# A new order, later stores, a second turning buffer and more exponentials on ScalarE in an attention-and-maxout kernel

## The chip, the cores and the metric

The kernel runs on one core of a Trainium2 chip. The core has a matrix engine (TensorE, PE in the profile, with PEld for its weight loads), three engines for elementwise work (VectorE or DVE, ScalarE or ACT, GpSimd or POOL), a queue engine that issues transfers (SyncE, SP) and 16 DMA engines. ACT can issue transfers too. The metric is the time of one execution in microseconds (us), as the median over runs.

## What is computed

Linear attention over 8 batches of 8 heads, 576 rows and 64 columns, and then a feed-forward layer on the 4608 x 512 result that takes the largest of three products:

```python
q_s = exp(q - max(q, axis=-1));  q_s /= sum(q_s, axis=-1) + 1e-09
k_s = exp(k - max(k, axis=2));   k_s /= sum(k_s, axis=2) + 1e-09
kv = einsum('bhsd,bhse->bhde', k_s, v)
x = einsum('bhsd,bhde->bhse', q_s, kv)          # rows b*576+s, columns h*64+e
h = maximum(maximum(x @ w1, x @ w2), x @ w3)    # 512 -> 768
out = h @ w_out                                 # 768 -> 512
```

## The kernel before

**Attention in pairs.** Two heads of one batch are a pair; pair n is batch n // 4 and heads 2(n % 4) and the next. There are 32. The first eight (batches 0 and 1) are turned by PE transposes (L533 to L558 for k, L713 for q). The other 24 are "late pairs". For one of these, k's column maximum is taken on DVE (L573 to L575), finished across partitions on POOL (L578), subtracted on DVE (L581), and exponentiated on ACT (L588). PE multiplies it with v (L603), and ACT writes the scaled 64 x 64 blocks to `bd` (L619). q arrives as `qt`, 128 x 576 with nine rows of 64 in each partition. DVE takes each row's maximum (L661), subtracts it (L663), ACT exponentiates all of it at once (L668), DVE adds up the rows (L670), inverts (L672, L673) and scales (L676). A block transpose on DVE writes `tb` (L681), and eight copies of 36 KB each by DMA put the blocks into `qT` (L694, some issued by SP and some by ACT). Then PE multiplies `qT` with `bd` (L740): this is the pair's product, a column block of x.

**The layer in stages.** Each fp32 weight is split into a high and a low fp32r part, and each product of the layer takes three matmuls of 128 x 512. The weights come in 24 slices, `wst` (L415), whose words are put together on DVE, POOL and ACT; the joined words are stored to DRAM as `wholes` (L462), and the split parts, which live in `gw`, as `scratch` (L1079 and L1084, three transfers for each of nine weight pairs: `kept`). The first three batches run as chunks of 512 rows with the weights in `gw` (L773, then L812). The other rows run as three double chunks with seven products where eight would be usual (L932, then L1043). Their weights are combinations: `sums` loads two `wholes` into `bench` (L1094), adds and subtracts on DVE (L1099, L1103) and stores to `scratch` (L1105). They come back one by one into a ring of 16 places in `gw` (L913). Their inputs are `raw` blocks of x, mixed on DVE and ACT (L869 to L880).

**What sets the order.** Nothing is scheduled by hand. Every piece of work is a generator of `Step`s with an engine, a cost and what it needs, frees and gives; `Streams.run` plays them on a model of the engines and takes, on each engine, the ready step of lowest rank. What it takes is issued in that order, and an engine then works through its list strictly in order. Constants near the top set ranks and model costs: `DMA_RATE` and `DMA_LANDS` for transfers, `AT`, `STEP`, `LATER` and so on for pairs, `SLICE…` for weights, `Q_BY_ACT` for the pairs whose row maximum goes into the exponential as ACT's bias. "turn" is the moment at which the first stage's buffers are given up and the late pairs' buffers exist.

## Time and profile before

| | |
|---|---|
| time, median of 3 runs | 708.24 us (700.74 to 711.59) |
| profiled execution, its own time | 706.54 us |
| its span, first to last instruction | 704.7 us |
| mean granted PE clock | 0.979 |
| DVE, ACT, POOL busy | 480.6, 264.1, 57.5 us |
| HBM read and written | 95.16 MB and 30.67 MB |

The profile is of one execution. Its engines' busy times are unions over instructions, and a matmul's own duration overlaps with that of the next, so PE's pace is read from how many matmuls fill a stretch, not from the mean of one. Releasers ("<-") say what ended a wait. "SPq" and "ACTq" are the issuing queues; a transfer's time to landing is counted from its issue. Eight semaphores go round among the transfers of SP and ACT, so a transfer also waits until the one that had its semaphore before has landed.

### The profile page before, as it was taken

How to read it: one execution, taken by the hardware profiler on the slowest of the kernel's cores; microseconds unless marked ns; L12 is line 12 of the kernel's file. 1: busy time of each engine (PE TensorE's matmuls, PEld its weight loads, DVE VectorE, ACT ScalarE, POOL GpSimd, SP SyncE). 2: the span in 40 equal slices, each digit the busy share in tenths (PEclk: the TensorE clock that was granted, in tenths of full speed). 3: DMA queues.
4: the chain of work that ended last, by engine and by line, in shares of the span. 5: the costliest groups of instructions: out<-in, count | busy, mean ns of one | idle time of the engine just before them, and what ended most of it. 6: DMA issues, size and time to landing. Idle time of an engine off the chain costs nothing.

```text
span 704.7 us, 9928 instructions
## 1 busy us (share of the span) xinstructions
PE 656.3 (93%) x3318; PEld 516.6 (73%) x3318; DVE 480.6 (68%) x865; ACT 264.1 (37%) x548; POOL 57.5 (8%) x68
## 2 busy tenths in 40 slices
PE   2859999999999788989988999999999999999997
PEld 1537877787777566767666777778888888888886
DVE  7988788589986778998868889624455913445421
ACT  4677855333443324453323336421112521111122
POOL 3222322110010000101000001000000000000000
PEclk9968999999999899999999999999999999999999
DMA  9999984416668976778878883346666316665012
GB/s 228 275 333 314 282 276 135 140 48 182 190 198 241 282 227 203 231 231 263 250 212 237 245 239 94 111 137 195 195 193 194 95 70 177 192 193 155 0 60 60
DMA packets 126162, 133.57 MB, mean 190 GB/s; under 512 B 57376, under 2 KB 88864, under 8 KB 124960
## 3 DMA queue, kind: packets, MB, share of 16 engines
q1 hardware_dynamic: 120800, 128.80, 62.0%
q10 hardware_dynamic: 5312, 4.16, 2.1%
q8 instruction: 26, 0.43, 0.3%
q14 instruction: 24, 0.20, 0.1%
HBM read 95.16 MB, written 30.67 MB: 179 GB/s over the span
## 4 chain that ended last, share of the span: by engine, by line
PE 73%; DMA 13%; DVE 6%; SPq 4%; ACT 2%; issue 1%; ACTq 0%; DVEq 0%
PE bank L932 33%; PE bank L773 18%; PE bank L1043 10%; DMA qT<-tb 6%; PE bank L812 4%; PE bank L740 3%; PE ps L603 2%; DMA wst<-in_moe_w_dram 2%; DVE tb L681 1%; DMA qt<-in_q_dram 1%; DMA vt<-in_v_dram 1%; DVE gw L880 1%; SPq L694 1%; DMA gw<-scratch 1%; DVE raw L876 1%
## 5 line engine op out<-in xcount | busy, mean ns | idle before, releaser
L932 PE MATMUL bank<-gw 128*128 128x512 f32 x1134 | 268.6, 395 | 3.0 <-ACT gw L878 1.1
L932 PEld LDWEIGHTS bank<-gw 128*128 128x128 f32 x1134 | 211.6, 188 | 51.6 <-issue 4.6
L773 PE MATMUL bank<-gw 128*128 128x512 f32 x432 | 112.6, 414 | 0.0
L773 PEld LDWEIGHTS bank<-gw 128*128 128x128 f32 x432 | 82.5, 195 | 21.5 <-issue 4.5
L1043 PE MATMUL bank<-oh,halves 128*128 128x512 f32 x288 | 89.2, 390 | 0.8 <-DVE halves L1021 0.8
L1043 PEld LDWEIGHTS bank<-oh,halves 128*128 128x128 f32 x288 | 54.1, 188 | 13.0 <-DVE halves L1021 1.2
L1043 PE MATMUL bank<-ol,halves 128*128 128x512 f32 x144 | 57.4, 398 | 0.0
L773 PE MATMUL bank<-x,gw 128*128 128x512 f32 x216 | 53.8, 403 | 0.0
L773 PEld LDWEIGHTS bank<-x,gw 128*128 128x128 f32 x216 | 40.1, 188 | 10.0 <-issue 1.4
L812 PE MATMUL bank<-oh,h 128*128 128x512 f32 x144 | 44.8, 393 | 0.0
L1021 DVE TENSOR_TENSOR halves<-hf,halves 128x768 fp32r<-128x768 f32 (+2 forms) x30 | 23.8, 798 | 30.1 <-ACT halves L1019 30.1
L578 POOL PARTITION_ALL_REDUCE kma<-km x24 | 20.0, 834 | 282.3 <-DVE ke L581 111.9
L740 PE MATMUL bank<-qT,bd 128*128 128x512 f32 x48 | 27.2, 650 | 15.8 <-DMA qT<-tb 11.9
L681 DVE STREAM_TRANSPOSE tb<-qt 128x576 f32<-128x576 f32 x24 | 30.4, 1265 | 7.0 <-DMA qT<-tb 4.6
L785 DVE TENSOR_TENSOR m<-bank,m 128x512 f32<-128x512 f32 x36 | 24.7, 686 | 11.4 <-PE bank L773 10.8
L812 PEld LDWEIGHTS bank<-oh,h 128*128 128x128 f32 x144 | 27.1, 188 | 6.8 <-issue 1.0
L812 PE MATMUL bank<-ol,h 128*128 128x512 f32 x72 | 32.0, 444 | 0.0
L1062 ACT COPY m<-bank 128x512 f32<-128x512 f32 x23 | 13.5, 586 | 48.9 <-PE bank L1043 40.1
L1043 PEld LDWEIGHTS bank<-ol,halves 128*128 128x128 f32 x144 | 27.0, 188 | 6.1 <-ACT qt L668 0.2
L989 ACT COPY m<-bank 128x512 f32<-128x512 f32 x18 | 10.5, 586 | 55.5 <-PE bank L932 45.4
L994 ACT COPY m<-bank 128x512 f32<-128x512 f32 x18 | 10.6, 587 | 55.3 <-PE bank L932 54.5
L996 DVE TENSOR_TENSOR m<-bank,m 128x512 f32<-128x512 f32 x18 | 12.4, 690 | 25.5 <-PE bank L932 21.4
(141 smaller groups left out, 876.3 us busy)
## 6 DMA issues: line engine op xcount, KB each, us to landing
gw<-scratch SPq DMA_DIRECT2D x189, 256.0 KB, 3.0
wst<-in_moe_w_dram SPq DMA_DIRECT2D x18, 512.0 KB, 5.8
scratch<-bench SPq DMA_DIRECT2D x9, 1024.0 KB, 4.9
out_dram<-m SPq DMA_DIRECT2D x32, 256.0 KB, 2.0
vt<-in_v_dram SPq DMA_DIRECT2D x56, 128.0 KB, 3.6
scratch<-gw SPq DMA_DIRECT2D x27, 256.0 KB, 4.8
qt<-in_q_dram SPq DMA_DIRECT2D x24, 288.0 KB, 3.7
kt<-in_k_dram SPq DMA_DIRECT2D x24, 256.0 KB, 4.0
```

The costliest lines, as they stand in the source:

```text
L578: nc.gpsimd.partition_all_reduce(kma, km, P, bass_isa.ReduceOp.max)
L603: nc.tensor.matmul(out=kv[r, :nv], lhsT=ke[rows, s, hh, :], rhs=self.vt[rows, hh, s, 0:nv], start=(s == 0), stop=(s == 4),)
L681: nc.vector.transpose(out=tb.rearrange("p e (c s) -> p s e c", s=QS), in_=self.qt.rearrange("p s (e c) -> p s e c", e=2))
L740: nc.tensor.matmul(out=xT, lhsT=self.terms[0], rhs=self.terms[1][:, cs], start=True, stop=True)
L773: nc.tensor.matmul(out=ps, lhsT=l[:, cc], rhs=r, start=(cc == 0 and t == 0), stop=(cc == NC - 1 and t == 2))
L785: nc.vector.tensor_max(out=m, in0=self.m.pop((j, i)), in1=m)
L812: nc.tensor.matmul(out=po, lhsT=l, rhs=r[:, j, :], start=(j == 0 and i == 0), stop=(j == NJ - 1 and i == 2))
L932: nc.tensor.matmul(out=po, lhsT=w[:, a, cc], rhs=x[:, b, cc], start=(first and cc == 0 and t == 0), stop=(cc == 1 and t == 2), skip_group_ ...
L996: nc.vector.tensor_sub(out=ma, in0=po("w"), in1=ma)
L1021: nc.vector.tensor_sub(out=hl, in0=src, in1=hh.bitcast(F32))
L1043: nc.tensor.matmul(out=po, lhsT=l, rhs=r[:, j, :], start=(j == 0 and i == 0), stop=(end and i == 2))
L1062: nc.scalar.copy(out=o, in_=po)
```

## The change

Costs and ranks of the planner are new numbers, and so the order of nearly every engine is new. Besides that, four things change in the code: (1) `kept` waits for "turn", so the 27 stores of split weights go out after the first stage instead of during it; (2) `tb` has two buffers instead of one; (3) k's maximum over its five row blocks is one reduction over a strided view instead of three maxima; (4) for the pairs in `Q_BY_ACT`, now 16 of them late pairs, q's negated row maximum goes to ACT as a bias, in nine calls that also give the row sums, so L663 and L670 fall away for them. Of the eight turned pairs six instead of three are done this way.

```diff
-DMA_LANDS = 2.0
-DMA_RATE, DMA_FIRST, DMA_AT_FIRST = 356.0, 0.62, 16.0
+DMA_LANDS = 1.8
+DMA_RATE, DMA_FIRST, DMA_AT_FIRST = 300.0, 0.74, 16.0
...
+LATE = (6.8, 43.0, 75.9, 91.3, 39.2, 63.1, 42.8, 12.9, 102.3, 84.5, 80.2, 91.4, 361.6, 375.8, 329.0, 379.5, 306.9, 342.2, 395.5, 316.4, 365.6, 408.8, 357.1, 341.6)
...
-FIRST_LOADS = 'vqwkQVKVwqvkQvkKqwqvwk'
+FIRST_LOADS = 'qVKKVqQwkwqvvQwvkqvkwk'
...
-Q_BY_ACT = (0, 4, 6)
+Q_BY_ACT = (1, 2, 4, 5, 6, 7, 8, 9, 11, 12, 13, 14, 17, 19, 20, 21, 22, 23, 26, 28, 30, 31)
...
-N_QT = 3
+N_QT, N_TB = 3, 2
+SPARE = 1.5
...
         def k_plain(self):
...
-            nc.vector.tensor_max(out=half, in0=kt[:, :, 0:2, :], in1=kt[:, :, 2:4, :])
-            nc.vector.tensor_max(out=kmv, in0=half[:, :, 0, :], in1=half[:, :, 1, :])
-            nc.vector.tensor_max(out=kmv, in0=kmv, in1=kt[:, :, 4, :])
+            nc.vector.tensor_reduce(
+                out=km.rearrange("p (h d) -> p h d", h=2), in_=kt.rearrange("p h s d -> p h d s"), op=ALU.max, axis=AX.X
+            )
...
-                nc.vector.tensor_reduce(out=qm, in_=rows3, op=ALU.max, axis=AX.X)
-                yield Step("V", dve(rows * D), port="V")
-                nc.vector.tensor_tensor(
-                    out=rows3, in0=rows3, in1=qm.unsqueeze(2).broadcast_to([P, rows, D]), op=ALU.subtract
-                )
+                nc.vector.tensor_reduce(out=qm, in_=rows3, op=ALU.max, axis=AX.X, negate=by_act)
+                if by_act:
+                    for s in range(0, QS, 3):
+                        yield Step("A", 3 * 0.33)
+                        for i in range(s, s + 3):
+                            nc.scalar.activation(
+                                out=rows3[:, i, :], in_=rows3[:, i, :], func=AF.Exp,
+                                bias=qm[:, i : i + 1], accum_out=qs[:, i : i + 1],
+                            )
...
-            tb = turn_pools[0].tile([P, 2, BL * QS], F32, name="tb", bufs=1)
+            tb = turn_pools[0].tile([P, 2, BL * QS], F32, name="tb", bufs=N_TB)
...
+            yield Step("-", SPARE, gives=("qT", n))
...
     def kept(f):
...
-        yield Step("S", 1.28, both, gives=("scratch", f, True, False, False), kb=512)
+        yield Step("S", 1.28, [*both, "turn"], gives=("scratch", f, True, False, False), kb=512)
```

`FIRST_LOADS` names the first transfers in order: a small letter is a pair's main rows of q, k or v, a capital the left-over rows of one or of three pairs, and `w` a weight slice. The first k of pair 0 was the fourth entry and is now the ninth.

**Where it shows: SP in the first stage.** Before, in the middle of the weight loads (`wst`) and of the loads for batch 1 (`kt`), stand stores of split weights (`scratch<-gw`), three by three:

```order
L462 DMA wholes_79<-m_441 128x512
L415 DMA wst_471<-in_moe_w2_dram 128x4x256
L1079 DMA scratch_78<-gw_73 128x2x256 x2
L1084 DMA scratch_78<-gw_73 128x2x256
L492 DMA kt1_91<-in_k_dram 128x4x64 x2
L415 DMA wst_547<-in_moe_w1_dram 128x4x256
L462 DMA wholes_79<-m_513 128x512
L1079 DMA scratch_78<-gw_73 128x2x256 x2
L1084 DMA scratch_78<-gw_73 128x2x256
```

Now they stand behind the last weight load, after "turn", around the first turned copies of pair 8 (`qT_1546`) and the loads of pairs 10 (`qt_1576`, `kt0`, `vt0`):

```order
L1110 DMA bench_1395<-wholes_79 128x1024
L1095 DMA scratch_78<-gw_73 128x2x256 x2
L1100 DMA scratch_78<-gw_73 128x2x256
L1095 DMA scratch_78<-gw_73 128x2x256 x2
L1121 DMA scratch_78<-bench_1395 128x2048
L1100 DMA scratch_78<-gw_73 128x2x256
L503 DMA kt0_90<-in_k_dram 128x2x256
L505 DMA kt0_90<-in_k_dram 64x2x64
L709 DMA qT_1546<-tb_1530 32x288 x4
L531 DMA qt_1576<-in_q_dram 128x576
L514 DMA vt0_92<-in_v_dram 128x4x64 x2
```

What moved are the 27 stores: 15 stand ahead of pair 8's turned copies on SP, 12 behind.

**SP at pair 14.** `qT_2221` is pair 14's turned q before. Ahead of its four copies on SP stand loads for other pairs, an output, two ring loads (`gw<-scratch`) and a load of 512 KB (`bench`):

```order
L506 DMA vt0_92<-in_v_dram 128x4x64 x2
L508 DMA vt0_92<-in_v_dram 64x2x64
L523 DMA qt_2173<-in_q_dram 128x576
L821 DMA out_0_dram<-m_2167 128x512
L495 DMA kt0_90<-in_k_dram 128x2x256
L497 DMA kt0_90<-in_k_dram 64x2x64
L913 DMA gw_73<-scratch_78 128x512 x2
L523 DMA qt_2215<-in_q_dram 128x576
L1094 DMA bench_1449<-wholes_79 128x1024
L694 DMA qT_2221<-tb_2207 32x288 x4
```

Now pair 14's is `qT_2244`, and its copies follow the first two ring loads at once:

```order
L709 DMA qT_2164<-tb_2145 32x288 x4
L837 DMA out_0_dram<-m_2177 128x512
L709 DMA qT_2164<-tb_2145 32x288 x2
L1121 DMA scratch_78<-bench_1395 128x2048
L514 DMA vt0_92<-in_v_dram 128x4x64 x2
L516 DMA vt0_92<-in_v_dram 64x2x64
L929 DMA gw_73<-scratch_78 128x512 x2
L709 DMA qT_2244<-tb_2232 32x288 x4
L531 DMA qt_2269<-in_q_dram 128x576
```

The q load and the 512 KB load that stood between ring loads and copies are gone from there.

**DVE at pair 14.** Before, from the row sums of pair 14 (`qt_2073`) to its block transpose (`tb_2207`), with steps of `sums` (`bench`) between:

```order
L670 TENSOR_REDUCE qs9_162<-qt_2073 128x9
L1099 TENSOR_TENSOR bench_1449<-bench_1449 128x256
L672 TENSOR_SCALAR qs9_162<-qs9_162 128x9
L673 RECIPROCAL qs9_162<-qs9_162 128x9
L1099 TENSOR_TENSOR bench_1449<-bench_1449 128x256
L676 TENSOR_TENSOR qt_2073<-qt_2073,qs9_162 128x576
L1099 TENSOR_TENSOR bench_1449<-bench_1449 128x256
L681 STREAM_TRANSPOSE tb_2207<-qt_2073 128x9x64
```

Now (`qt_2037`, `tb_2232`), the sums come from ACT and the subtraction has gone too:

```order
L687 TENSOR_SCALAR qs9_162<-qs9_162 128x9
L688 RECIPROCAL qs9_162<-qs9_162 128x9
L691 TENSOR_TENSOR qt_2037<-qt_2037,qs9_162 128x576
L620 TENSOR_SCALAR rk_2216<-ps_130 128x1
L621 RECIPROCAL rk_2216<-rk_2216 128x1
L667 TENSOR_REDUCE qm9_163<-qt_2162 128x9
L696 STREAM_TRANSPOSE tb_2232<-qt_2037 128x9x64
```

L670 has no counterpart for this pair, and three of `sums`' steps are no longer in between. The number of matmuls on PE is the same; of the layer's 2430, 390 stood ahead of pair 8's product and 411 do now, and from there to the product of pair 31 it was 1011 and is 1008.

More of the change, by code (lines that the diff above doesn't have):

```diff
@@ L47 @@
 N_TMP = 7
-SUMS_AT, SUMS_STEP = 60.0, 8.0
-LATER = 400.0
-N_QT = 3
+N_QT, N_TB = 3, 2
+SPARE = 1.5
 LEFT_OF = (0, 1, 6, 2, 3, 4, 5)
@@ L222, in issue @@
         end = t + c
-        self.clock[e] = end
+        if e != "-":
+            self.clock[e] = end
         if e in step.port:
@@ L378, in linear_attention_then_maxout_ffn @@
     st = Streams(
-        {"pf": banks_of_gates, "pa": banks_of_heads, "ring": RING, "ws": 1, "sums": 1, "halves": 2, "ps": 4, "keT": 1, "hp": NJ, "tmp": N_TMP, "ke": 2, "qe": 2, "qf": 1, "qt": 2, "tb": 1, "qT": N_QT},
+        {"pf": banks_of_gates, "pa": banks_of_heads, "ring": RING, "ws": 1, "sums": 1, "halves": 2, "ps": 4, "keT": 1, "hp": NJ, "tmp": N_TMP, "ke": 2, "qe": 2, "qf": 1, "qt": 2, "tb": N_TB, "qT": N_QT},
         {
@@ L382, in linear_attention_then_maxout_ffn @@
             "ring": range(len(PRODUCTS) * ((B + 1 - PLAIN) // 2)),
+            "qf": range(TURNED * NP),
             **{r: range(TURNED * NP, B * NP) for r in ("qt", "tb", "qT")},
@@ L520, in q_load @@
             else:
-                yield Step("S", 0.64, ["turn"], gives=("q", self.n), take=[("qt", self.n)], kb=288)
+                yield Step("S", 0.4, ["turn"], gives=("q", self.n), take=[("qt", self.n)], kb=288)
                 self.qt = turn_pools[0].tile([P, QS, D], F32, name="qt", bufs=2)
@@ L595, in k_steps @@
             yield Step(
-                "T", 0.9, [("v", n), self.ago("xmm", 0), self.ago("xmm", 1)], take=last, free=[("ke", n)], gives=("kv", n)
+                "T", 0.5, [("v", n), self.ago("xmm", 0), self.ago("xmm", 1)], take=last, free=[("ke", n)], gives=("kv", n)
             )
@@ L660, in q_steps @@
                 rows3 = self.qt
-                nc.vector.tensor_reduce(out=qm, in_=rows3, op=ALU.max, axis=AX.X)
-                yield Step("V", dve(rows * D), port="V")
-                nc.vector.tensor_tensor(
-                    out=rows3, in0=rows3, in1=qm.unsqueeze(2).broadcast_to([P, rows, D]), op=ALU.subtract
-                )
+                nc.vector.tensor_reduce(out=qm, in_=rows3, op=ALU.max, axis=AX.X, negate=by_act)
[7 more added lines that the diff above has]
+                            )
+                else:
+                    yield Step("V", dve(rows * D), port="V")
+                    nc.vector.tensor_tensor(
+                        out=rows3, in0=rows3, in1=qm.unsqueeze(2).broadcast_to([P, rows, D]), op=ALU.subtract
+                    )
             if not by_act:
@@ L688, in q_steps @@
                         "SA", 0.6, take=[("qT", n)] if i == e == 0 else (), free=[("tb", n)] if end else (),
-                        gives=("qT", n) if end else None, kb=36,
+                        kb=36,
                     )
@@ L817, in second @@
             nc.scalar.copy(out=o, in_=po)
-            yield Step("S", 0.64, kb=256, free=[("tmp", (c, "y", t))], rank=-1000.0)
+            yield Step("S", 0.4, kb=256, free=[("tmp", (c, "y", t))], rank=-1000.0)
             rows = out[c * S : c * S + CH, :]
@@ L911, in ring_loads @@
                     after += self.block_free(k * CH // NW)
-                yield Step("S", 0.64, after, take=[("ring", k)], gives=("ringed", k), kb=256)
+                yield Step("S", 0.36, after, take=[("ring", k)], gives=("ringed", k), kb=256)
                 nc.sync.dma_start(out=ring[k % RING].bitcast(F32).rearrange("p t a b -> p (t a b)"), in_=scratch[f, :, a, :])
@@ L1063, in second @@
             if chunk < B:
-                yield Step("S", 0.64, kb=256, free=[("tmp", (c, "y", t))], rank=-1000.0)
+                yield Step("S", 0.4, kb=256, free=[("tmp", (c, "y", t))], rank=-1000.0)
                 nc.sync.dma_start(out=out[chunk * S + tq * P : chunk * S + (tq + 1) * P, :], in_=o)
@@ L1089, in sums @@
         h = P * 2
-        yield Step("S", 0.64, ["turn"] + [("whole", n) for n in duos[0].tiles_of(f)], take=[("ws", f)], kb=512)
+        yield Step("S", 0.4, ["turn"] + [("whole", n) for n in duos[0].tiles_of(f)], take=[("ws", f)], kb=512)
         ws = bench[0][:, 4 * CH :].rearrange("p (u n) -> p u n", u=2)
@@ L1218, in linear_attention_then_maxout_ffn @@
         else:
-            at, step = FIRST + CHUNK * (b - 1) + 14.0 * g, 1.0
-        if b >= PLAIN + 2:
-            at = LATER + NP * (b - PLAIN - 2) + g
-        ahead = 12.0 if b else 0.0
+            at, step = LATE[p.n - TURNED * NP], 1.0
+        ahead = LOADS_AHEAD if b else 0.0
         st.add(p.k_load(), at - ahead)
@@ L1244, in linear_attention_then_maxout_ffn @@
     for f in range(NG // 2):
-        st.add(kept(f), SUMS_AT + SUMS_STEP * f)
-        st.add(sums(f), SUMS_AT + SUMS_STEP * f)
+        st.add(kept(f), KEPT[f])
+        st.add(sums(f), SUMS[f])
     for d, duo in enumerate(duos):
```

22 lines of the change are left out of this document (13 added, 9 removed).

## The prediction

> **What bounds the kernel.** I read the head of the page first, then busy time by stage, then the chain of waits.
>
> ```profile
> span 704.7 us, 9928 instructions
> PE 656.3 (93%) x3318; PEld 516.6 (73%) x3318; DVE 480.6 (68%) x865; ACT 264.1 (37%) x548; POOL 57.5 (8%) x68
> ```
>
> PE is busy 93% of the span, so 704.7 us can only shrink by what PE loses. Where it loses, by stage (us, PE, PEld, DVE, ACT and POOL busy with instructions, granted clock, DMA share, GB/s):
>
> ```profile
> 0.00:60.00 60.00, 36.08 (x192) 24.62 (x193) 50.42 (x117) 38.68 (x117) 16.38 (x24) 0.86 1.00 281
> 60.00:160.00 100.00, 100.00 (x528) 79.25 (x527) 76.75 (x152) 55.49 (x129) 23.57 (x23) 1.00 0.62 190
> 100.00:160.00 60.00, 60.00 (x299) 47.26 (x298) 43.85 (x87) 25.43 (x51) 11.85 (x15) 1.00 0.41 122
> 160.00:466.00 306.00, 285.94 (x1567) 219.35 (x1566) 247.90 (x453) 119.98 (x222) 17.50 (x21) 0.98 0.71 212
> 466.00:700.00 234.00, 234.00 (x1034) 193.36 (x1032) 105.11 (x144) 49.62 (x80) 0.00 (x0) 1.00 0.49 139
> ```
>
> PE is full from 60 to 160 and from 466 to 700. It loses in the first 60 us, when DMA is saturated (share 1.00) and DVE is 84% busy, and in the 306 us in which the late pairs are made, where DVE is 81% busy. A busy PE need not be at its pace, so I count the second loss from the chain (start, us, what):
>
> ```profile
> 160.87 0.73 PE ps L603 x20
> 161.60 1.05 PE bank L740 x2
> ...
> 465.40 0.86 PE bank L740 x2
> 466.25 0.17 PE ps L740 x2
> ...
> 467.48 80.32 PE bank L932 x354
> ```
>
> A dense layer matmul takes 80.32 / 354 = 0.227 us, a product 0.86 + 0.17 = 1.03, a pair's k times v 0.73. Between the first late product (pair 8, 161.6) and the last (pair 31, 465.4) lie 303.8 us. PE's order has 1011 layer matmuls, 23 products and 22 k-times-v there: 229.5 + 23.7 + 16.1 = 269.3 us. So 34.5 us are lost there. What PE waits for is in one row, and the worst case, pair 14, in the chain:
>
> ```profile
> L740 PE MATMUL bank<-qT,bd 128*128 128x512 f32 x48 | 27.2, 650 | 15.8 <-DMA qT<-tb 11.9 <-DMA gw<-scratch 3.4 <-ACT bd L619 0.5
> 220.98 1.20 DVE tb L681
> ...
> 223.90 6.06 DMA gw<-scratch
> ...
> 230.59 2.38 DMA qT<-tb
> 232.97 0.24 issue
> 233.21 2.05 PE bank L740 x2
> ```
>
> The product waits for the turned copies. Their source is ready at 222.2, but the product starts at 233.2, 11.0 us later. Four of the copies are issued by SP, and SP was here (start, us):
>
> ```profile
> 223.29 1.05 SPq L913 DMA_DIRECT2D gw<-scratch  x2
> 225.82 0.33 SPq L523 DMA_DIRECT2D qt<-in_q_dram  x1
> 226.64 1.41 SPq L1094 DMA_DIRECT2D bench<-wholes  x1
> 228.71 2.47 SPq L694 DMA_DIRECT2D qT<-tb  x4
> ```
>
> So the queue in front of the copies, not the copies, makes them late, and DVE's load decides how early their source can be.
>
> **The change, part by part.** *Exponentials on ACT.* For 16 late pairs L663 and L670 go, and L668 becomes nine calls:
>
> ```profile
> L663 DVE TENSOR_TENSOR qt<-qt,qm 128x576 f32<-128x576 f32 x24 | 17.9, 751 | 0.1
> L670 DVE TENSOR_REDUCE qs<-qt 128x9 f32<-128x576 f32 x24 | 17.8, 744 | 5.3 <-ACT qt L668 5.2
> L668 ACT ACTIVATE qt<-qt 128x576 f32<-128x576 f32 x24 | 16.3, 684 | 32.8 <-DVE qt L663 24.9 <-DMA qT<-tb 6.2 <-DVE rk L614 1.1
> 45.45 1.77 ACT qe L648 x10
> ```
>
> DVE loses 16 x (0.751 + 0.744) = 23.9 us. Five such calls with their sums took 1.77 us, so nine take 3.19, and ACT gains 16 x (3.19 - 0.68) = 40 us. ACT is busy 120 of 306 us in that stage, so it goes to about 160 of 306, in pieces of three calls (1.06 us): that delays a neighbour's copy out of PSUM by 1 us, which the four to six banks in turn should absorb. Three more turned pairs take another 3 x (0.816 + 0.816) = 5 us from DVE in the first stage:
>
> ```profile
> L653 DVE TENSOR_TENSOR qe<-q,qm 128x640 f32<-128x640 f32 x4 | 3.3, 816 | 0.0
> L670 DVE TENSOR_REDUCE qs<-qe 128x10 f32<-128x640 f32 x5 | 4.1, 816 | 0.5 <-ACT qe L668 0.4
> ```
>
> *k's maximum.* Three maxima become one reduction of 640 elements, read with a step of 64 elements:
>
> ```profile
> L573 DVE TENSOR_TENSOR kh<-kt 128x256 f32<-128x256 f32 x24 | 9.9, 415 | 5.7 <-DMA kt<-in_k_dram 5.7
> L574 DVE TENSOR_TENSOR km<-kh 128x128 f32<-128x128 f32 x24 | 7.0, 292 | 1.6
> L575 DVE TENSOR_TENSOR km<-km,kt 128x128 f32<-128x128 f32 x24 | 7.0, 292 | 2.4 <-DMA kt<-in_k_dram 1.6
> L631 DVE TENSOR_REDUCE qm<-q 128x10 f32<-128x640 f32 x8 | 6.4, 810 | 0.4 <-DMA q<-in_q_dram 0.4
> L681 DVE STREAM_TRANSPOSE tb<-qt 128x576 f32<-128x576 f32 x24 | 30.4, 1265 | 7.0 <-DMA qT<-tb 4.6 <-DMA vt<-in_v_dram 2.1
> ```
>
> It replaces 1.00 us a pair. No row shows that form. The nearest is L631, the same reduction of 640 elements read in line, 0.81 us; the far end is L681, which writes with a step, 1265 / 576 = 2.2 ns an element, so 1.41 us for 640. Per pair that is between -0.19 and +0.41, in all -4.6 to +9.8 us of DVE; I take 0.81. The Trainium skill, "SBUF — State Buffer" (§ Door 1: The DMA port swizzle), speaks against it: SBUF has 16-byte lines, and an access that crosses to a new line pays a penalty, which every element of this view does. It states no price; by the rule DVE would move toward the far end, and the sum with it at most to the third rival's 698. The writing side of L681 agrees (2.2 ns an element against L631's 1.3); no run here shows a reduction read in this way.
>
> *Two turning buffers.* L681 waited 4.6 us for the copies out of the one `tb`; those waits go. What is late next is `qT`, which keeps three buffers.
>
> *The stores.* 27 transfers of 256 KB leave the first stage: 7.1 MB, at the 281 GB/s of the saturated first 60 us 25 us of all DMA engines. They land in the hole that the row 100:160 shows (share 0.41, so 35 us of free DMA time), and a little beyond. Nothing needs them before the ring loads, but 15 stand ahead of pair 8's copies. With the other transfers after "turn" that is 8.0 MB or 28 us, and PE, with 21 layer matmuls more ahead of that product, has work until 161.6 + 21 x 0.227 = 166.4. The q load of pair 8 was issued at 135.8:
>
> ```profile
> 135.78 0.83 SPq L523 DMA_DIRECT2D qt<-in_q_dram  x2
> ...
> scratch<-gw SPq DMA_DIRECT2D x27, 256.0 KB, 4.8
> ```
>
> 135.8 + 28 and the landing of the last, 4.8 at most after its issue, come to 164 to 169, just at the deadline; the earlier turn that a lighter first stage gives is what makes room, so I count no loss and keep up to 11 us for the range (8.0 MB at the 190 GB/s of 60:160).
>
> *The start.* DVE has less to do and no stores come after 34 us, but the first k is issued ninth instead of fourth, behind five more issues of 0.64 us, so 3 us later, and everything in the first 20 us hangs on it:
>
> ```profile
> 2.24 1.36 SPq L1134 DMA_DIRECT2D k<-in_k_dram  x2
> 3.64 0.64 SPq L1141 DMA_DIRECT2D q<-in_q_dram  x1
> ...
> 33.68 1.25 SPq L1079 DMA_DIRECT2D scratch<-gw  x2
> ```
>
> Bounds: 3 us worse with the order as only change, up to 5 + 2 us better if the half-clock time (0.14 of 36.08 us) goes and DVE's saving is felt. I take 2 us better.
>
> *The middle.* A product's time from a ready `tb` to its start was 11.0 us at pair 14. Counted in the order from the last PE result that DVE waits for, and with the durations above, `tb` used to be ready only 6 to 10 us of PE work ahead of its product for pairs 8 to 19 and 3.5 to 6 for pairs 21 to 24. Now it is 8 to 20 us, and over 15 from pair 20 on. With 11 us needed at worst, only pairs 13, 18 and 19 (10, 8, 8.5) can be short, by 1 + 3 + 2.5 = 6.5 us. After the last product ahead of the seven-product stage there are 39 matmuls (8.9 us) instead of 12 (2.7), which covers the mixing. I leave as much again, 5.5 us, for loads and ring places that come late. So 12 of the 34.5 us stay, and 22.5 go. Matmul counts by stage shift but the total doesn't, and the end is PE alone, so it costs the same.
>
> *Sum.* 704.7 - 2 - 22.5 = 680.2 us of span. The profiled execution took 706.54, 1.8 more, and the median of the runs shown is another 1.7 above it: 680.2 + 3.5 = 684 us.
>
> **The rivals.**
> *Slower: the stores crowd the queue.* Transfers wait for their turn of eight semaphores, so 8.0 MB ahead of pair 8 hold SP up, and 12 more stores meet the loads of pairs 10 to 12. For it: DMA is busy 0.71 over the stage already. Against it: the 35 free us. If the 25 us came onto PE's path and left the old waits standing, 708 + 25 = 733. It decides once pair 8's product is over 38 us behind its place in PE's work, because then the other gains (24.5) plus 14 are used up.
> *The waits stay.* The new order has late copies elsewhere, since SP still runs ring loads that wait for PE between the copies, as at 223.29 above. With three quarters of the middle's loss kept and no gain at the start, 708 - 8 = 700, no change.
> *The strided read costs.* If the 0.6 us a pair above my value fell on PE's path in all 24 pairs, 684 + 14 = 698. DVE's new lead speaks against it.
> *The start gains as well.* DMA with 25 us less to carry and DVE with 5 less bring 5 us more, and the middle loses only 5: 684 - 5 - 7 = 672.
>
> **How the numbers follow.** The forecast has 0.48, the better start 0.17, the waits that stay 0.22, the strided read 0.06, the crowded queue 0.07. The forecast's own range is 675 to 693. The range 668 to 704 takes in the better start, the strided read and most of the case in which the waits stay, and leaves the crowd out. Two per cent (14 us, below 694) is about what a measurement of this kernel can tell from no change. Faster: 0.48 + 0.17 = 0.65; within it: 0.22 + 0.06 = 0.28; slower: 0.07.
>
> **What would show it.** The share of qT copies in the chain, 6% before, should fall to under 2%:
>
> ```profile
> PE bank L932 33%; PE bank L773 18%; PE bank L1043 10%; DMA qT<-tb 6%; PE bank L812 4%; PE bank L740 3%; PE ps L603 2%; DMA wst<-in_moe_w_dram 2%; DVE tb L681 1%; DMA qt<-in_q_dram 1%; DMA vt<-in_v_dram 1%; DVE gw L880 1%; SPq L694 1%; DMA gw<-scratch 1%; DVE raw L876 1%
> ```
>
> In the stages, PE should near 100% busy in 160:466 and DVE fall below 75%; L740's wait should be under 5 us; the new reduction should read about 0.81 us; DMA share in 100:160 should rise from 0.41 to over 0.7; the first matmul should start about 3 us later, and pair 8's product between 161 and 169. The prediction is wrong if PE starts the dense last stretch later than 450 us, or if pair 8's product stands and waits.

## The result, and the profile after

| | before | after |
|---|---|---|
| time, median | 707.96 us (700.74 to 711.94) | 700.54 us (696.13 to 706.22) |
| ratio, 95% interval | | 0.992 (0.989 to 0.995) |
| span of the profiled execution | 704.7 us | 694.3 us |
| product of pair 8 / of pair 31 in the chain | 161.6 / 465.4 | 163.3 / 459.5 |

The kernel got 1% faster, 7.4 us by the medians, where 24 were forecast. A profile shows one execution, here the shortest of the changed kernel's (696.13 us), while those of e5 and e6 below took 7 and 5 us more than their medians. The head of its page and busy time by stage (columns as before):

```profile
span 694.3 us, 10133 instructions
PE 652.2 (94%) x3318; PEld 514.4 (74%) x3318; DVE 460.7 (66%) x774; ACT 310.5 (45%) x881; POOL 65.8 (9%) x69
```

```profile
0.00:60.00 60.00, 36.56 (x207) 24.80 (x207) 46.40 (x110) 42.77 (x149) 14.88 (x23) 0.91 0.84 226
60.00:160.00 100.00, 99.81 (x545) 79.06 (x544) 77.72 (x149) 66.94 (x197) 24.63 (x24) 1.00 0.65 207
100.00:160.00 60.00, 59.81 (x331) 46.89 (x330) 44.66 (x84) 36.40 (x113) 11.65 (x14) 1.00 0.65 206
160.00:466.00 306.00, 291.87 (x1584) 225.51 (x1583) 234.35 (x378) 152.85 (x462) 26.30 (x22) 0.99 0.74 223
```

The stage of the late pairs gained only 6 us of PE work (291.87 for 285.94), although DVE there has 13.6 us less to do and ACT 33 us more. The groups that answer to those of before, and the chain's shares:

```profile
L756 PE MATMUL bank<-qT,bd 128*128 128x512 f32 x48 | 26.0, 623 | 10.1 <-DMA qT<-tb 7.4 <-ACT bd L625 2.7
L579 DVE TENSOR_REDUCE km<-kt 128x128 f32<-128x640 f32 x24 | 31.0, 1293 | 20.5 <-DMA kt<-in_k_dram 19.9 <-POOL kma L584 0.6
L667 DVE TENSOR_REDUCE qm<-qt 128x9 f32<-128x576 f32 x24 | 17.9, 746 | 15.5 <-DMA qt<-in_q_dram 15.2
L672 ACT ACTIVATE qt<-qt,qm 128x64 f32<-128x64 f32 x144 | 48.4, 340 | 19.4 <-DVE qm L667 9.2 <-DMA qT<-tb 6.3 <-DVE qs L687 2.0
L696 DVE STREAM_TRANSPOSE tb<-qt 128x576 f32<-128x576 f32 x24 | 30.4, 1265 | 0.4
```

```profile
PE bank L948 34%; PE bank L789 16%; PE bank L1059 14%; PE bank L828 5%; PE bank L756 3%; DMA qT<-tb 3%; DMA qt<-in_q_dram 2%; PE ps L609 2%; DMA kt<-in_k_dram 2%; ACT qe L654 1%; SPq L1150 1%; PE ps L756 1%; SPq L1153 1%; DVE tb L696 1%; SP
```

The block transpose no longer waits for its buffer (0.4 us for 7.0), but the product still waits 10.1 us, and DVE stands 35 us at the loads of k and q. Before, it stood 19 us there: 7.3 at k's (L573 and L575) and 12.1 at q's:

```profile
L661 DVE TENSOR_REDUCE qm<-qt 128x9 f32<-128x576 f32 x24 | 17.9, 748 | 12.3 <-DMA qt<-in_q_dram 12.1
```

Pair 14 is again the worst place. The chain there (start, us, what), with pair 8's and pair 31's products at its ends:

```profile
163.32 0.86 PE bank L756 x2
...
201.17 4.94 DMA qT<-tb
...
207.52 3.08 DMA qt<-in_q_dram
...
215.32 4.13 DMA kt<-in_k_dram
...
219.55 1.29 DVE km L579
...
222.93 1.11 DVE tb L696
...
224.62 1.19 ACTq L709
...
226.65 4.51 DMA qT<-tb
...
234.48 2.55 DMA qT<-tb
...
237.27 2.04 PE bank L756 x2
...
459.45 0.86 PE bank L756 x2
```

Copies, a q load, a k load and copies again follow one another, each issued only when a queue gets to it. SP's list shows what stood ahead of pair 14's four copies there, and SP's longest wait:

```profile
223.60 2.09 SPq L514 DMA_DIRECT2D vt<-in_v_dram  x2
230.48 0.62 SPq L516 DMA_DIRECT2D vt<-in_v_dram  x1
231.22 0.99 SPq L929 DMA_DIRECT2D gw<-scratch  x2
232.32 2.74 SPq L709 DMA_DIRECT2D qT<-tb  x4
SPq L516 <- DMA qT<-tb: 4.7, 1, 4.7
```

The block was ready at 224.0. ACT issued its four copies of it from 224.1 on. SP stood 4.7 us ahead of a v load, until the first of those copies had landed at 230.4: in the records the two transfers have the same one of the eight semaphores. Only behind that v load and two ring loads came SP's own copies.

From pair 8's product to pair 31's it is 459.45 - 163.32 = 296.1 us, 303.8 before. With the prices of the prediction PE's work in between is 1008 x 0.227 + 23 x 1.03 + 22 x 0.73 = 268.6 us, so 27.6 are lost where 12 were forecast. 14.1 of them stand in PE's wait rows from 165 to 460 us. This span is the measure of all runs below.

### The profile page after: what moved, and what is told of

Read it like the earlier page. It is cut to its first block, busy times and chain, and to the rows that moved or that the text cites. A ratio compares the mean times of both kernels' runs of the same rounds, so it can differ in the third digit from the quotient of the medians.

```text
span 694.3 us, 10133 instructions
## 1 busy us (share of the span) xinstructions
PE 652.2 (94%) x3318; PEld 514.4 (74%) x3318; DVE 460.7 (66%) x774; ACT 310.5 (45%) x881; POOL 65.8 (9%) x69
## 4 chain that ended last, share of the span: by engine, by line
PE 78%; DMA 7%; DVE 4%; SPq 4%; ACT 4%; issue 2%; ACTq 1%; DVEq 0%
PE bank L948 34%; PE bank L789 16%; PE bank L1059 14%; PE bank L828 5%; PE bank L756 3%; DMA qT<-tb 3%; DMA qt<-in_q_dram 2%; PE ps L609 2%; DMA kt<-in_k_dram 2%; ACT qe L654 1%; SPq L1150 1%; PE ps L756 1%; SPq L1153 1%; DVE tb L696 1%; SPq L709 1%
## 5 line engine op out<-in xcount | busy, mean ns | idle before, releaser
L672 ACT ACTIVATE qt<-qt,qm 128x64 f32<-128x64 f32 x144 | 48.4, 340 | 19.4 <-DVE qm L667 9.2
L584 POOL PARTITION_ALL_REDUCE kma<-km x24 | 27.8, 1159 | 279.2 <-DVE km L579 108.0
L789 PE MATMUL bank<-x,gw 128*128 128x512 f32 x216 | 52.4, 399 | 0.0
L579 DVE TENSOR_REDUCE km<-kt 128x128 f32<-128x640 f32 x24 | 31.0, 1293 | 20.5 <-DMA kt<-in_k_dram 19.9
L756 PE MATMUL bank<-qT,bd 128*128 128x512 f32 x48 | 26.0, 623 | 10.1 <-DMA qT<-tb 7.4
L801 DVE TENSOR_TENSOR m<-bank,m 128x512 f32<-128x512 f32 x36 | 24.5, 682 | 13.9 <-PE bank L789 11.2
```

The source lines that it names most:

```text
L579: nc.vector.tensor_reduce(out=km.rearrange("p (h d) -> p h d", h=2), in_=kt.rearrange("p h s d -> p h d s"), op=ALU.max, axis=AX.X)
L584: nc.gpsimd.partition_all_reduce(kma, km, P, bass_isa.ReduceOp.max)
L672: nc.scalar.activation(out=rows3[:, i, :], in_=rows3[:, i, :], func=AF.Exp, bias=qm[:, i : i + 1], accum_out=qs[:, i : i + 1],)
L756: nc.tensor.matmul(out=xT, lhsT=self.terms[0], rhs=self.terms[1][:, cs], start=True, stop=True)
L789: nc.tensor.matmul(out=ps, lhsT=l[:, cc], rhs=r, start=(cc == 0 and t == 0), stop=(cc == NC - 1 and t == 2))
L801: nc.vector.tensor_max(out=m, in0=self.m.pop((j, i)), in1=m)
```

## The experiments

Edits are to the changed kernel unless it is said otherwise, and they leave the plan's steps, and so the order of the rest, as they are. "Before" ran beside each at 705.3 to 709.1 us.

| run | us | ratio to before (95%) | pair 8 to 31, us |
|---|---|---|---|
| changed kernel | 700.5 | 0.989 to 0.995 | 296.1 |
| e1 product waits for no copy | 699.9 | 0.984 to 0.995 | 297.6 |
| e2 no late stores | 694.4 | 0.977 to 0.986 | 292.3 |
| e3 stores early | 695.0 | 0.978 to 0.988 | 288.1 |
| e4 k loads early | 708.8 | 1.001 to 1.007 | 305.8 |
| e5 three maxima | 700.2 | 0.987 to 0.993 | |
| e6 exponentials at once | 707.9 | 0.996 to 1.004 | 305.6 |
| e7 seven of nine store groups early | 692.4 | 0.974 to 0.986 | 288.8 |
| e8 the same and three maxima | 691.4 | 0.973 to 0.982 | 288.8 |
| e9 pairs feed PE nothing | 698.3 | 0.982 to 0.992 | 295.4 |
| e10 before, rows on ACT | 718.2 | 1.008 to 1.020 | 315.3 |
| e11 e8, copies by SP alone | 701.7 | 0.990 to 0.997 | 298.1 |
| e12 k load not awaited | 700.5 | 0.990 to 0.995 | 298.9 |
| e13 k and q loads not awaited | 701.0 | 0.988 to 0.995 | 299.2 |
| e14 no copies | 677.6 | 0.955 to 0.960 | 275.9 |
| e15 small copies | 697.6 | 0.983 to 0.987 | 292.5 |
| e16 e8, ACT's copies by GpSimd | 678.6 | 0.957 to 0.965 | 275.8 |
| e17 e8, all copies by GpSimd | 685.9 | 0.964 to 0.974 | 277.5 |
| e18 changed kernel, ACT's copies by GpSimd | 683.0 | 0.956 to 0.967 | 277.3 |

**e1: PE's wait for the copies taken away.**

```diff
-            self.terms = (bds[self.m], self.qT)
+            self.terms = (bds[self.m], None)
...
+                rhs = ident[:, 0:w] if u else ident.unsqueeze(1).broadcast_to([P, 4, P])
```

> The changed kernel, but the late pairs' products multiply a constant instead of the turned q, so that they wait for no copy; the copies still run. This leaves out the late pairs' x, and with it the right result. Theory 1 (the copies hold PE): between the products of pair 8 and pair 31, 27.6 us are lost in the changed kernel's profile. 10.9 us of these stand directly ahead of five products, and some 2 us more follow them at half clock. If the copies are the cause, the loss falls to about 14 us and the time to 687 us. Theory 2 (what feeds the copies is late too: k loads, VectorE, the blocks bd): PE then waits for bd instead, the loss stays over 22 us and the time over 695 us.

699.9 us: theory 2. PE now stood at k times v, for ACT to free the place in PSUM (group by line):

```profile
L609 PE MATMUL ps<-vt,ke 128*64 128x65 f32 (+2 forms) x560 | 23.3, 227 | 9.1 <-ACT left L764 6.8 <-DMA vt<-in_v_dram 2.3
```

Here the wait that the row named was only where PE met the delay; with that wait gone PE met one of ACT's instead.

**e2, e3: the stores left out, and issued early.** In e2 the three `dma_start`s of each group are gone, and the ring loads read other words of the same size. In e3 each group of three stores is issued as soon as it is split, ahead of the steps that wait for "turn":

```diff
-        yield Step("S", 1.28, [*both, "turn"], gives=("scratch", f, True, False, False), kb=512)
+        yield Step("-", 0.0, both)
         for l in range(2):
...
-        yield Step("S", 0.64, both, gives=("scratch", f, False, True, False), kb=256)
...
+        yield Step("S", 1.28, [*both, "turn"], gives=("scratch", f, True, False, False), kb=512)
+        yield Step("S", 0.64, both, gives=("scratch", f, False, True, False), kb=256)
```

> The changed kernel with its planned order, but without the 27 stores of split weights (7.1 MB); the ring loads that would read them read other words of the same size, so the last five batches come out wrong. Theory 1 (the moved stores crowd SP's queue and the DMA engines, and make the copies and loads of pairs 10 to 16 late): the loss between the products of pair 8 and 31 falls from 27.6 to 20 us or less, most of it before 250 us, and the time to 693 us. Theory 2 (the stores land in idle DMA time, the order itself leaves too little time): the loss stays at 25 to 28 us and the time within 2 us of 700.5.

> The changed kernel with its planned order, but each store of split weights is issued as soon as the split is ready, in the first stage, as in the kernel before; its place in the plan stays empty. Theory 1 (the moved stores crowd the middle): the middle loses 20 us instead of 27.6; the first stage loses 3 us more, which is what it won with the change; time 696 us. Theory 2 (the stores cost nothing where they are): the middle stays, the start loses 3 to 6 us, time 704 to 707 us.

694.4 and 695.0 us: the stores behind the turn do cost the late pairs something. Without them the span is 3.8 us shorter, and 23.7 us stay lost, between e2's two theories. With them early it is 8.0 us shorter, as theory 1 of e3 says. Part of the 8.0 is only moved: pair 8's product came at 169.1 there, 5.8 us later than in the changed kernel, and pair 31's at 457.2, 2.2 us earlier (457.3 in e2). In e3 PE lost in the first stages instead. Busy time there, and the chain at the place:

```profile
60.00:160.00 100.00, 97.40 (x528) 76.88 (x527) 75.58 (x145) 66.71 (x197) 24.59 (x24) 0.98 0.71 223
```

```profile
109.99 5.57 DMA wst<-in_moe_w_out_dram
...
115.67 0.66 ACT wx L433
...
116.32 0.11 ACT left L759
...
116.48 0.27 PE ps L733
```

A late weight load, among the last stores, held ACT, and ACT held PE.

**e4: k loaded as soon as its buffer is free.**

```diff
-                    yield Step("S", 0.64, [prev], kb=256)
+                    yield Step("-", 0.0, [prev])
                     nc.sync.dma_start(out=self.kt[:, :, 0:4, :], in_=main_rows(k, self.b, self.hs))
...
+                    yield Step("S", 0.64, kb=256)
```

> The changed kernel with its planned order, but each late pair's k is loaded as soon as its buffer is free (after the subtraction of the pair two before), 3 to 12 us earlier than now. In the changed kernel's profile VectorE stands 20 us in all ahead of the k maximum, 19.9 of them for k's load, with all its later work behind it. Theory 3 (the k loads come too late for VectorE, which works strictly in order, and so the block transposes and the copies are late): VectorE's wait ahead of the k maximum falls under 8 us, the loss between the products of pair 8 and 31 from 27.6 to 22 us or less, time 695 us. Theory 1 or 2 of the stores and the order: the wait goes elsewhere, time within 2 us of 700.5, or slower by up to 4 since SP now stands at these loads.

708.8 us, 8 slower, more than any theory had. DVE's wait for k fell as theory 3 says, but the product's rose:

```profile
L580 DVE TENSOR_REDUCE km<-kt 128x128 f32<-128x640 f32 x24 | 31.1, 1294 | 7.3 <-DMA kt<-in_k_dram 7.3
L757 PE MATMUL bank<-qT,bd 128*128 128x512 f32 x48 | 27.0, 644 | 15.0 <-DMA qT<-tb 10.7 <-ACT raw L760 2.6 <-ACT bd L626 1.7
```

This fits k loads that, put earlier in SP's list, hold back the copies behind them; no run separates it further.

**e5: three maxima again.**

```diff
-            nc.vector.tensor_reduce(
-                out=km.rearrange("p (h d) -> p h d", h=2), in_=kt.rearrange("p h s d -> p h d s"), op=ALU.max, axis=AX.X
-            )
+            nc.vector.tensor_max(out=half, in0=kt[:, :, 0:2, :], in1=kt[:, :, 2:4, :])
+            nc.vector.tensor_max(out=kmv, in0=half[:, :, 0, :], in1=half[:, :, 1, :])
+            nc.vector.tensor_max(out=kmv, in0=kmv, in1=kt[:, :, 4, :])
```

> The changed kernel in its planned order, with k's maximum again taken by three maxima in place of the one strided reduction. The strided reduction took 1.293 us, the three took 1.00 us, so VectorE has 7 us less to do, all in the stretch of the late pairs; GpSimd's reduction, which took 1.16 us beside the strided one, should be back at 0.83. Theory A (VectorE's time is on the path there): the span between the products of pair 8 and pair 31 falls from 296.1 to about 292 us, time 696 to 697 us. Theory B (VectorE stands 20 us for k's loads, so what it saves it waits): its wait ahead of the first of the three grows by 3 us or more, the time stays within 1.5 us of 700.5.

700.2 us: no difference. Only durations are read from its profile: 0.420, 0.292 and 0.292 us, 1.00 in sum, for 1.293. GpSimd's reduction took 0.82 us for 1.16, as expected. The 7 us of DVE are worth nothing here, as theory B says of the time; whether its wait for k grew, as B also says, is left open.

**e6: the row-wise exponentials undone.**

```diff
                 if by_act:
+                    nc.vector.tensor_tensor(out=rows3, in0=rows3, in1=qm.unsqueeze(2).broadcast_to([P, rows, D]), op=ALU.add)
                     for s in range(0, QS, 3):
                         yield Step("A", 3 * 0.33)
-                        for i in range(s, s + 3):
-                            nc.scalar.activation(...)
+                        if s == 0:
+                            nc.scalar.activation(out=rows3, in_=rows3, func=AF.Exp)
...
+            if by_act and not self.turned:
+                nc.vector.tensor_reduce(out=qs, in_=rows3, op=ALU.add, axis=AX.X)
```

> The changed kernel in its planned order, with the row-wise exponentials of the 16 late pairs undone: VectorE subtracts the row maximum and adds up the rows again, ScalarE takes the exponential in one call. VectorE gets 24 us more to do, ScalarE 40 us less. Theory A (VectorE's time is on the path): the late pairs' products come later, the span from pair 8's product to pair 31's goes from 296.1 to 302 us or more, time 706 us or more. Theory B (ScalarE, which issues part of the copies and stands in order behind the row-wise calls, is what delays the copies): the span falls by 2 us or more, time 698 or less. Theory C (loads, stores and SP's queue decide): within 2 us of 700.5.

707.9 us: theory A. In this order taking 24 us off DVE is worth 7 us, although it puts the longer calls on ACT (7.4 by the medians; by the ratios of e5 and e6, which ran together, 1.0% or 7.2).

**e7, e8: most stores early, and three maxima with them.** As e3, but the last two groups (the weight pairs 6 and 8) stay behind the turn.

```diff
+        late = f in (6, 8)
+        if not late:
+            yield Step("-", 0.0, both)
+            stored(f, na, nb, 0, 3)
...
```

> The changed kernel in its planned order, with the stores of seven of the nine weight pairs issued as soon as they are split and those of the last two left behind the turn. With all nine early the middle took 8.0 us less (288.1 for 296.1), and pair 8's product came 4 us later than in the run without any of these stores, since the last weight loads at 110 us, behind stores, held ScalarE and then PE. Theory 1 (the first seven land in idle DMA time, the last two are what costs at 110 us): pair 8's product back at 164 to 165, the middle at 288 to 291, time 691 to 692 us. Theory 2 (two groups behind the turn are enough to crowd the loads of pairs 9 to 12): the middle at 293 or more, time 695 us or more.

> The kernel with seven of nine store groups early, and three maxima in place of the strided reduction. Theory A (with the stores out of the way VectorE's time is on the path): 2 to 4 us faster than with the stores alone. Theory B (k's loads decide when VectorE can begin): within 1.5 us of it.

692.4 and 691.4 us: theory 1, and theory B of e8. PE is full again ahead of pair 8 in e7, with DMA shares of 0.93 and 0.71:

```profile
0.00:60.00 60.00, 36.80 (x201) 25.28 (x202) 44.84 (x106) 41.31 (x144) 14.93 (x23) 0.91 0.93 261
60.00:160.00 100.00, 99.43 (x542) 78.28 (x541) 78.11 (x149) 67.48 (x201) 24.67 (x24) 1.00 0.71 225
```

So seven groups cost the first stage nothing that can be seen (pair 8's product comes at 165.3, and at 165.0 in e2, without any), and the move of the stores took back 7 to 9 us of what the rest of the change brings (e7 against the changed kernel, e8 against e5).

**e9: nothing of the pairs feeds PE.** As e1, with `ident` in both products of a late pair.

```diff
-                        out=kv[r, :nv], lhsT=ke[rows, s, hh, :], rhs=self.vt[rows, hh, s, 0:nv],
+                        out=kv[r, :nv], lhsT=ke[rows, s, hh, :] if turned else ident[:, 0:D],
+                        rhs=self.vt[rows, hh, s, 0:nv] if turned else ident[:, 0:nv],
```

> The changed kernel in its planned order; both matrix products of each late pair (k times v, and q times the result) multiply constants, while all their loads, VectorE, ScalarE and GpSimd work, copies and stores run on. This leaves out the late pairs' results. TensorE waits then for nothing that the late pairs prepare, only for its banks, the mixed inputs and the ring. It gives the floor of what an order could reach. Theory F1 (the 12 us that the forecast left in the middle were about what no order removes): the span from pair 8's product to pair 31's falls from 296.1 to 280 us, time about 684 us. Theory F2 (much of what was counted as lost is TensorE's own, around each product): the span stays above 286 us, time above 690 us. Theory F3 (waits are all there was): the span falls to 272 us or less, time 677 us.

698.3 us and 295.4. By its numbers theory F2, but the run does not measure a floor, as e14 shows: PE waited for ACT to free PSUM (waits of PE from 165 to 460: us, times, longest).

```profile
PE ps L609 <- ACT left L764: 7.3, 3, 3.5
```

**e10: the kernel before, with rows on ACT alone.**

```diff
+                if not self.turned and rowwise:
+                    for i in range(QS):
+                        nc.scalar.activation(
+                            out=rows3[:, i, :], in_=rows3[:, i, :], func=AF.Exp,
+                            bias=qm[:, i : i + 1], accum_out=qs[:, i : i + 1],
+                        )
```

> The kernel before in its own order, with one thing added: the 16 late pairs that the change gives to ScalarE take their exponentials by rows there, so VectorE has 24 us less to do and ScalarE 40 us more. In the changed kernel undoing this cost 7.4 us. Theory A (VectorE's time is on the path in either order): 700 to 703 us against 707. Theory B (only the new order can use it; in the old one the queue ahead of the copies decides, and nine calls take longer for one pair than one): 706 us or more.

718.2 us against 705.3, ratio 1.014: 10 to 13 us slower, so theory B, and worse than it said. PE's longest waits in that stage:

```profile
PE bank L751 <- DMA qT<-tb: 12.9, 7, 2.9
PE bank L943 <- ACT gw L889: 3.6, 1, 3.6
```

Before, PE waited 11.9 us for copies and 1.1 for ACT's `gw` in that stage. What is worth 7 us in the new order costs 10 or more in the old. That it is the nine calls where the plan had given ACT one is likely, but not shown.

**e11: e8 with all copies in SP's queue.**

```diff
-                    (nc.sync if queue == "S" else nc.scalar).dma_start(
+                    nc.sync.dma_start(
```

> The kernel of the run with seven store groups early and three maxima, with all turned copies issued by SP; about half of them stood in ScalarE's queue, at the same places of the plan. In the changed kernel's late stretch ScalarE's work waited 36 us behind copies of its own queue that waited for an earlier copy to land. Theory D (these stops on ScalarE delay what PE waits for): ScalarE's waits behind copies go, time 2 us or more below that run. Theory E (SP, which needs 0.6 us for each issue, is then the later one): 2 us or more above it, and PE waits longer for the copies.

701.7 us, 10 more than e8: theory E. PE waits longer for the copies, here first e11, then e8:

```profile
PE bank L758 <- DMA qT<-tb: 8.8, 5, 3.8
PE bank L758 <- DMA qT<-tb: 2.7, 2, 1.9
```

ACT without its stops is worth less than what SP's longer queue costs.

**e12, e13: no one waits for the loads of k, then of k and q.**

```diff
-                out=km.rearrange("p (h d) -> p h d", h=2), in_=kt.rearrange("p h s d -> p h d s"), op=ALU.max, axis=AX.X
+                out=km.rearrange("p (h d) -> p h d", h=2), in_=consts[0].rearrange("p h s d -> p h d s"), op=ALU.max, axis=AX.X
...
-                in0=kt,
+                in0=consts[0],
```

e13 takes q's maximum, exponential and subtraction from the same constant, and q's load goes into a k buffer.

> The changed kernel in its planned order; VectorE takes the late pairs' k maximum and subtracts it from a constant, while k's loads run on into their buffers, so nothing waits for them. This leaves out the late pairs' k. In the changed kernel VectorE stood 19.9 us at the k maximum for k's load. Theory L (k's loads, late behind other transfers, stop VectorE with all its later work, and so blocks, copies and PSUM space for PE): the span from pair 8's product to pair 31's falls from 296.1 to 290 us or less, time 694 us or less. Theory M (q's loads, at which VectorE stands 15.2 us, take k's place): the wait at the q maximum grows by 5 us or more, time 697 us or more.

> As the run before, and q's maximum and exponentials are taken from a constant too, while q's loads run on into a k buffer. This leaves out the late pairs' q as well. The 19.9 and 15.2 us of standing at both loads go. Theory L: the span from pair 8's product to pair 31's falls to 284 us or less, time 688 us or less, so about what was forecast. Theory N (the copies' own queue, which stays as it is, holds PE by itself): the span stays at 290 us or more, time 694 us or more.

700.5 and 701.0 us: theories M and N. In e12 DVE stood at q instead, in e13 PE at the copies (waits of each engine in that stage):

```profile
DVE qm L667 <- DMA qt<-in_q_dram: 31.8, 14, 4.1
```

```profile
PE bank L758 <- DMA qT<-tb: 10.5, 5, 2.5
```

So the late loads are not what holds PE by itself.

**e14, e15: no copies, and small ones.** e14 is e1 without the `dma_start` of L709; e15 copies 32 of 288 columns:

```diff
-                        out=self.qT[r : r + BL, BL * QS * (i % 2) : BL * QS * (i % 2 + 1)],
-                        in_=tb[BL * i : BL * (i + 1), e, :],
+                        out=self.qT[r : r + BL, BL * QS * (i % 2) : BL * QS * (i % 2) + 32],
+                        in_=tb[BL * i : BL * (i + 1), e, 0:32],
```

> The changed kernel with its plan's order; the late pairs' products multiply a constant and the 192 turned copies (36 KB each, 6.9 MB, about 0.6 us of a queue for each issue) are not issued at all. This leaves out the late pairs' x. With the copies running and only their result unused it was 699.9 us. Theory Q (SP's and ScalarE's queues of transfers, which every load, copy and store passes in order, are the bound of this stretch): 688 us or less, the span from pair 8's product to pair 31's 284 us or less, and VectorE's standing at the k and q loads falls under half of 35 us. Theory R (something else that all these runs share, the order on VectorE and ScalarE themselves): 696 us or more.

> As the run before, but all 192 copies are issued, each with 32 of its 288 columns, so with a ninth of the bytes. Theory Q1 (it is the number of issues and their waits for one another, not the bytes): as with whole copies, 696 us or more, while the run without copies is at 688 or less. Theory Q2 (it is the bytes that the DMA engines carry): as without copies, 690 us or less.

677.6 us without the copies, 697.6 with small ones: theories Q and Q1. Without copies PE is full over the whole stage, and DVE's standing at the loads of k and q is gone (e14, busy time and groups):

```profile
160.00:456.00 296.00, 296.00 (x1629) 232.52 (x1629) 240.99 (x387) 155.08 (x464) 25.98 (x22) 1.00 0.68 208
```

```profile
L579 DVE TENSOR_REDUCE km<-kt 128x128 f32<-128x640 f32 x24 | 31.0, 1292 | 0.8 <-POOL kma L584 0.6 <-DMA kt<-in_k_dram 0.2
L667 DVE TENSOR_REDUCE qm<-qt 128x9 f32<-128x576 f32 x24 | 17.7, 739 | 0.0
```

With small copies it is not, though the DMA engines carry no more than in e14 (0.68, 206 GB/s). Its busy time, and its copies' median time to landing from 165 to 240 us, with that of the changed kernel's below:

```profile
160.00:456.00 296.00, 284.34 (x1558) 221.69 (x1557) 234.21 (x379) 150.56 (x454) 25.49 (x22) 0.99 0.68 206
```

```profile
qT<-tb SPq DMA_DIRECT2D x26, 4.0 KB, 2.0
qT<-tb ACTq DMA_DIRECT2D x21, 4.0 KB, 3.3
```

```profile
qT<-tb SPq DMA_DIRECT2D x26, 36.0 KB, 2.1
qT<-tb ACTq DMA_DIRECT2D x21, 36.0 KB, 3.7
```

A ninth of the bytes takes 0.1 us off SP's 2.1 and 0.4 off ACT's 3.7, and 2.3 us off the kernel's time of e1. So the number of transfers in two queues holds this stage, not what they carry. e14 takes away SP's issues, ACT's and their waits at once; it does not say which of these counts.

**e16, e17, e18: a third queue.** In e16 the copies that stood in ACT's list are issued by GpSimd at the same places; e17 gives it all copies; e18 is the changed kernel with only this edit.

```diff
-                    (nc.sync if queue == "S" else nc.scalar).dma_start(
+                    (nc.sync if queue == "S" else nc.gpsimd).dma_start(
```

> The kernel with seven store groups early and three maxima (691.4 us), with the copies that ScalarE issued given to GpSimd at the same places of the plan: a third queue, which has only the 24 reductions in this stretch, and whose transfers go round semaphores of their own. All of the computation stays. Theory Q1 (the number of issues in the two queues, and their waits for one another, is the bound): 686 us or less, PE's waits between pair 8 and pair 31 under 5 us. Theory S (GpSimd issues slowly, or a copy there stands behind a reduction that waits for a k maximum): 695 us or more.

> As the run before, with all 192 copies given to GpSimd, so that SP has 0.6 us for each of the other 96 less to do and no copy stands between its loads. Theory Q1: as good as the run before or better, 678 to 686 us. Theory S: eight copies one after the other on one queue take longer than four on each of two, the products come later than in the run before, 690 us or more.

> The changed kernel, all else as it is (stores behind the turn, strided reduction), with ScalarE's copies given to GpSimd. Theory Q1 (two queues and one round of semaphores for all transfers were what kept the 27.6 us in the middle): the span from pair 8's product to pair 31's falls from 296.1 to 280 us or less, time 685 us or less, so about the forecast. Theory T (the late stores hold it by themselves, even so): span 288 us or more, time 692 us or more.

678.6, 685.9 and 683.0 us: theory Q1. e16 computes everything and is 0.961 of before (0.957 to 0.965). Its stage is full, its product waits for nothing, and PE has no wait row at all from 165 to 460 us:

```profile
160.00:456.00 296.00, 296.00 (x1630) 232.55 (x1629) 235.54 (x432) 154.67 (x464) 58.17 (x105) 1.00 0.74 221
```

```profile
L758 PE MATMUL bank<-qT,bd 128*128 128x512 f32 x48 | 24.6, 594 | 0.0
L711 POOL DMA_DIRECT2D qT<-tb x91 | 45.9, 505 | 137.4 <-DVE tb L698 22.6 <-DVE hf L987 19.5 <-issue 12.6
```

e17 is slower, at the upper end of what Q1 gave, and scatters more (680.6 to 688.0); its profile shows one wait of PE for copies, 0.6 us, so why is not shown. e18 is 4.4 us above e16, but before was 2.4 us slower beside it too, and the ratios (0.962 and 0.961) don't tell the two apart: with a third queue the late stores and the strided read cost little or nothing, 1.5 us by the spans. It did what its theory Q1 says (277.3 us, 683.0).

## Why the prediction failed

- **The middle: wrong, and this is the step that failed.** It said that 11 us at worst lie between a ready `tb` and its product, that the new order has `tb` ready 8 to 20 us ahead, and that 5.5 us more do for loads that come late; so 12 us stay. 27.6 stayed. Pair 14's transposed block was ready at 224.0 (222.93 + 1.11) and its product began at 237.3, 13.2 us later. The lead was counted in PE's work, as if DVE and ACT waited for PE alone; both also wait for transfers, 35 us at k's and q's loads, and transfers wait in SP's list, where a v load's wait for one of ACT's copies alone took 4.7 us at pair 14. Taking single waits away (e1, e9, e12, e13) only moved the time to the next wait. Taking out the 192 copies left 275.9 - 268.6 = 7.3 us, and giving about half of them a third queue 7.2 (e16) and 8.7 (e18). In e16 no wait is left, so these 7 us are what the count by dense matmuls leaves out of PE's own work, and not waits that an order could remove; the prediction had them in its 34.5. What the changed kernel lost beyond them and the 14.1 us of waits, some 6 us by difference, is in part a lower clock: granted was 0.50 from 237 to 243 us, behind the wait at pair 14, which is worth some 3 us, where e16 has 1.00 over the stage. The rest is not accounted for. So the 12 us could be had, and the 684 with them (e18: 683.0), but by a third queue added to this order, not by the order alone.
- **The rivals.** The time of "the waits stay" came out (700), in part by luck: it had no gain at the start, where 3.1 us were seen, and 2.7 us of the time are only the profiled execution being short. That the loss stays was right (27.6 of 34.5 us). Its reason, ring loads between the copies, was too narrow: v loads stood there too, and it is the transfers of both lists together that count. "The stores crowd the queue" had the mechanism and the wrong size: pair 8's product stood for nothing, as forecast, but the move of the stores took 7 to 9 us (e7, e8), not 25; which of the 15 ahead of its copies and the 12 behind cost that was not separated.
- **The stores and the start.** That the first stage would gain from stores leaving is not shown: in e7 seven groups are back there, and pair 8's product comes at 165.3. In the changed kernel's profile the start gained 3.1 us, near the 2 forecast, but runs whose edits touch only the late pairs put that product between 163.3 and 170.8 (168.8 in e18, 170.8 in e6), so a gain of 2 us is inside the scatter. The first matmul came 2.5 us later, as forecast.
- **Exponentials on ACT.** DVE's saving was real, and the part was worth 7 us (e6). Left out was that the same part costs 10 us or more in an order that was not made for it (e10).
- **k's maximum.** I took 0.81 us; it is 1.293, near the far end of 1.41. The rule of the Trainium skill, "SBUF — State Buffer" (§ Door 1: The DMA port swizzle), that an access which crosses to a new line pays, agrees with this and would have been the better guide. It cost no time that can be seen (e5, e8), so the third rival falls.
- **Two turning buffers.** Their wait went, 7.0 to 0.4 us. One buffer in the new order wasn't tried.
- **The rest.** Between span and median lay 6.2 us instead of 3.5, since the profiled execution was the shortest. So the miss of 16.5 us is 15.6 in the middle and 2.7 here, less 1.1 at the start and 0.4 at the end (and 0.3 of rounding). Of the signs named, DMA share in 100:160 (0.65), DVE's share (77%), the product's wait (10.1) and the copies' share of the chain (3%) all stopped short of the forecast, and the dense stretch began after 450 us, which was named as proof against.

What stays open: how much of a third queue's help is issuing time, and how much is that its transfers wait in a round of semaphores of their own (the records give those of GpSimd in e16 eight others than those of SP). Both count. In e11 SP stands only 4 us for transfers from 165 to 460 us, but it issues 409 and is 10 us later than e8. From e8 to e16 SP's issues take the same time (183 and 184 us in that stretch), but it stands 8 us for transfers instead of 37, and ACT 1 instead of 30 (sums of the wait rows). Not run was the kernel before with a third queue, so what the new order is worth once there is room to issue is not known either.

The Trainium skill, "DMA: Bandwidth & Descriptors" (§ Issuing engines are not separate DMA queues), says that issuing from several engines saves only the issuing engine's time. e16 agrees in that hardly more is carried (221 GB/s for 215 in e8, 160 to 456 us), but that time, with its waits in order, was worth some 12 us here (e8 to e16: 12.8 by the medians, 11.5 by the ratios).

## What to carry to other kernels

When several engines wait a little for different transfers, count the transfers in each issuing list and take a whole class of them away in an experiment, before reading the wait rows as causes: a single wait removed only shows the next one. Small transfers cost their place in the list here, not their bytes, so spread them over engines that have little else in order, though not all over one (e11, e17), and put large ones that nobody needs soon where the lists are short, but not among loads that an engine is waiting for. The worth of moving work to another engine belongs to the order it is in: the same exponentials gave 7 us in one and cost 10 or more in the other.

## What was not expected of the hardware

- A copy between partitions of 4 KB landed in 2.0 us, one of 36 KB in 2.1 (SP, same stretch).
- A DVE maximum over 640 fp32 elements took 1.293 us read with a step of 64 elements, and 0.810 read in line.
- GpSimd issued 91 copies at 0.505 us each beside its reductions, which still took 0.79 us each (19.0 us for 24).
- Kernels that differ only in the late pairs reached pair 8's product 7.5 us apart (163.3 to 170.8, changed kernel and e6), with a granted clock of 0.91 and 0.85 in the first 60 us.
- GpSimd's reduction took 1.16 us in the changed kernel and 1.15 in e14, with k's maximum read with a step, and 0.82 in e5 and 0.79 in e16, with three maxima. Why is not shown.
